# Loading q in two half-tile transfers with 512-byte runs, and restoring the token order in a PSUM copy

## The chip, the cores and the metric

One core of a Trainium2 chip runs the program. The metric is device time in microseconds. Executions of one kernel on one chip that count as fast spread by up to 1.5 percent. A run more than 1.5 percent above the fastest of its kernel is marked slow. The changed kernel and every experiment were timed in rounds beside the kernel before on the same chip. A ratio is taken from fast runs of the same rounds, so it is not quite the ratio of the medians quoted beside it. The bracket behind a ratio is its 95% interval.

## The reference

Linear attention with a decay per head (4 batches, 8 heads, 768 tokens, 64 elements), then a feed-forward layer on 3072 tokens. The reference works in blocks of 64 tokens; the kernel gets the same result in chunks of 128.

```python
for b in range(nb):
    intra = np.einsum('bhic,bhjc->bhij', qb, kb) * Dmask[None]
    intra = np.einsum('bhij,bhjd->bhid', intra, vb)
    inter = np.einsum('bhid,bhde->bhie', qb * lam_pow[None], kv_state)
    out[:, :, sl] = intra + inter
    kv_state = lam_block[None, :, None, None] * kv_state + np.einsum('bhsd,bhse->bhde', kb_dec, vb)
...
x = np.ascontiguousarray(attn_out.transpose(0, 2, 1, 3)).reshape(B * S, H * D)
h = x @ w_in                    # 512 -> 2048, then a smooth ReLU, then @ w_out
```

## The kernel before

There are 24 chunks. SyncE loads k, q and v of a chunk as [128 tokens, 8 heads, 64] float32. A head's 64 elements are 256 contiguous bytes in memory, so a load is 1024 runs of 256 bytes. GpSimd scales and casts q and k; q is turned by PE (first chunks) or by a DMA transpose; PE makes scores, applies them to v and adds the state; ScalarE copies the result as x^T into SBUF; then the two large matmul layers follow, six stages of 512 tokens.

```python
def f_load(c, x, wait):
    t = ld.tile([128, H, D], F32, name=f"x{x}f", tag=f"x{x}f")
    b, s0 = c // NCB, (c % NCB) * C
    d = nc.sync.dma_start(out=t, in_=(q, k, v)[x][b, :, s0:s0 + C, :].rearrange("h p d -> p h d"))
...
def f_x(c):                                     # x^T of a chunk, from PSUM
    nc.scalar.copy(out=xT[sx][:, :, off:off + C], in_=pot[c])
...
# the planner: each operation is entered with its cost; run_plan sorts all engines' instructions by it
add(("ld", it, x), "SP", 590, lambda ...: f_load(i, x, wait), [...], due=pos_ * 1e-3, dma=1190)
```

The order of every engine's instructions is fixed before the run, by a list scheduler inside the kernel that works with entered costs. "SP, 590" is the issue on SyncE in nanoseconds, "dma" the transfer. At run time each engine follows its order and waits where data are late: in the profile of this kernel ScalarE waits 16.4 us for v.

## Time and profile before

| | before |
|---|---|
| time, median of 2 runs | 229.81 us (228.67 to 230.96) |
| profiled span | 225.5 us |
| PE busy | 205.6 us, so 19.9 idle |
| 256 KB q load | 24 issues, median 4.4 us from issue to landing |
| k loads from chunk 10 on (the expectations below call it chunk 8) | (146.50 - 69.65) / 13 = 5.91 us apart |

The page's engine line gives busy time, share of the span and number of instructions; the stretches give, for each window, its length and every engine's busy time. The idle time of PE is what can be won or lost. The lines themselves stand in the prediction below.

### The profile page before, as it was taken

What the parts mean: (1) busy time and instruction counts of PE and PEld (TensorE: products, weight loads), DVE (VectorE), ACT (ScalarE), POOL (GpSimd) and SP (SyncE); (2) the same over time, 40 slices, a digit from 0 to 9 for tenths busy, and PEclk for the clock granted to TensorE, in tenths of its full rate; (3) what the DMA queues carried; (4) which work ended last, traced back from release to release, by engine and by line L of the source; (5) the groups of instructions that cost most, each with busy time, mean ns of one, the idle gap of its engine ahead of it and who ended that gap; (6) DMA issues with size and microseconds to landing.
All of it is one profiled execution on the core that took longest, in us unless ns stands there. A gap on an engine that the chain in (4) does not pass through costs nothing.

```text
span 225.5 us, 4385 instructions
## 1 busy us (share of the span) xinstructions
PE 205.6 (91%) x1733; PEld 123.4 (55%) x1760; DVE 144.2 (64%) x218; ACT 123.6 (55%) x220; POOL 61.0 (27%) x65
## 2 busy tenths in 40 slices
PE   0497989999999989689999999999999999999992
PEld 0376634765888577567664554545545544444441
DVE  7687399978498948567655956856656564554300
ACT  3346867544678285546757575676655444455121
POOL 6543560056034332423342542361000000000000
PEclk9999999999999999999999999999999999999998
DMA  6999999999898797999999999999011001110212
GB/s 121 216 218 170 195 189 202 200 223 196 212 202 158 182 215 169 205 173 204 225 196 237 214 166 233 232 211 211 0 49 47 24 22 49 47 47 16 77 67 77
DMA packets 102837, 34.38 MB, mean 152 GB/s; under 512 B 95136, under 2 KB 99744, under 8 KB 102816
## 3 DMA queue, kind: packets, MB, share of 16 engines
q1 hardware_dynamic: 97920, 29.90, 70.4%
q0 software_dynamic: 4752, 4.19, 12.2%
q8 instruction: 14, 0.23, 0.5%
q14 instruction: 7, 0.06, 0.1%
q10 hardware_dynamic: 144, 0.00, 0.0%
HBM read 27.27 MB, written 6.29 MB: 149 GB/s over the span
## 4 chain that ended last, share of the span: by engine, by line
PE 57%; SPq 3%; DMA 2%; issue 1%; ACT 1%; ACTq 0%
PE py L365 27%; PE ph L332 23%; PE po L305 3%; DMA x2f<-in_v_dram 2%; PE ps L285 2%; SPq L406 1%; PE po L302 1%; PE pu L266 1%; SPq L256 1%; SPq L260 1%; ACT vi L235 0%; ACT osb L370 0%; PE pt L285 0%; ACTq L370 0%
## 5 line engine op out<-in xcount | busy, mean ns | idle before, releaser
L332 PE MATMUL ph<-xT,w_in_sb 128*128 128x128 bf16 (+1 forms) x741 | 92.5, 268 | 1.9 <-ACT xT L312 1.0
L365 PE MATMUL py<-w_out_sb,gT 128*128 128x512 bf16 x368 | 92.6, 379 | 1.0 <-issue 0.2
L340 ACT ACTIVATE r<-ph,one 128x512 bf16<-128x512 f32 (+2 forms) x96 | 64.6, 678 | 47.7 <-PE ph L332 38.4
L332 PEld LDWEIGHTS <-w_in_sb 128*128 128x128 bf16 x752 | 52.5, 98 | 29.0 <-issue 2.2
L365 PEld LDWEIGHTS <-gT 128*128 128x128 bf16 x384 | 35.7, 98 | 38.8 <-DVE gT L356 0.2
L348 DVE TENSOR_SCALAR t<-r 128x1024 bf16<-128x1024 bf16 x48 | 25.2, 526 | 42.7 <-ACT r L340 42.7
L356 DVE TENSOR_TENSOR gT<-w,t 128x1024 bf16<-128x1024 bf16 x48 | 39.8, 828 | 1.6
L231 POOL TENSOR_TENSOR ks<-x1f,tab_k 128x512 bf16<-128x512 f32 x20 | 22.1, 1103 | 62.0 <-DMA x1f<-in_k_dram 48.9
L351 DVE TENSOR_TENSOR w<-r,t 128x1024 bf16<-128x1024 bf16 x48 | 37.2, 775 | 1.5
L231 POOL TENSOR_TENSOR qs<-x0f,tab_q 128x512 bf16<-128x512 f32 x24 | 28.5, 1189 | 25.7 <-DMA x0f<-in_q_dram 25.3
L235 ACT CAST vi<-x2f 128x512 bf16<-128x512 f32 x24 | 14.8, 616 | 16.5 <-DMA x2f<-in_v_dram 16.4
L295 DVE TENSOR_TENSOR sc<-ps,causal 128x512 bf16<-128x512 f32 x20 | 13.8, 689 | 13.6 <-PE pt L285 13.6
L370 ACT COPY osb<-py 128x512 f32<-128x512 f32 x24 | 14.1, 586 | 15.1 <-PE py L365 13.4
L305 PE MATMUL po<-sc,vi 128*128 128x128 bf16 x192 | 19.2, 226 | 0.2
L312 ACT CAST xT<-po 128x512 bf16<-128x512 f32 x24 | 14.0, 585 | 7.2 <-PE po L305 6.6
L270 ACT CAST ubd<-pu 64x256 bf16<-64x256 f32 x40 | 14.6, 364 | 5.3 <-PE pu L266 5.0
L305 PEld LDWEIGHTS <-vi 128*128 128x128 bf16 x192 | 15.2, 102 | 2.3 <-issue 0.6
L302 PE MATMUL po<-qT,ubd 128*128 128x128 bf16 x80 | 15.1, 224 | 0.0
L295 DVE TENSOR_TENSOR sc<-pt,causal 128x512 bf16<-128x512 f32 x20 | 13.6, 680 | 0.0
L266 PE MATMUL pu<-vi,ks 128*128 128x128 bf16 x80 | 8.4, 232 | 2.4 <-ACT vi L235 2.3
L241 PE MATMUL pt<-ident,ks 128*128 128x128 bf16 x24 | 3.1, 266 | 8.0 <-DVE ks L231 7.8
L266 PEld LDWEIGHTS <-ks 128*128 128x128 bf16 x80 | 6.4, 105 | 5.5 <-issue 3.1
(48 smaller groups left out, 87.4 us busy)
## 6 DMA issues: line engine op xcount, KB each, us to landing
x1f<-in_k_dram SPq DMA_DIRECT2D x24, 256.0 KB, 4.8
x0f<-in_q_dram SPq DMA_DIRECT2D x24, 256.0 KB, 4.4
x2f<-in_v_dram SPq DMA_DIRECT2D x24, 256.0 KB, 4.6
out_dram<-osb SPq DMA_DIRECT2D x24, 256.0 KB, 2.6
w_out_sb<-in_moe_w_out_dram POOLq DMA_DIRECT2D x4, 512.0 KB, 13.3
w_in_sb<-in_moe_w_in_dram POOLq DMA_DIRECT2D x3, 512.0 KB, 6.6
w_in_sb<-in_moe_w_in_dram POOLq DMA_DIRECT2D x2, 256.0 KB, 5.0
kT<-ks SPq DMA_TRANSPOSE x18, 4.2
```

Source lines behind the costliest of these rows:

```text
L231: eng.tensor_tensor(t, qkv_ld[c, x], _bc(tab[:, c % NCB, :], 2, D), op=AX.mult)
L235: nc.scalar.copy(out=v_out(vi[c % NV]), in_=qkv_ld[c, 2].rearrange("p (a b) d -> p a b d", b=2))
L266: nc.tensor.matmul(pu[0][:, hp, :], lhsT=pair(ks[c], hp), rhs=v_pair(vi[c % NV], hp), start=(c % NCB == 0 and hp == 0), stop=True, skip_gr ...
L295: nc.vector.tensor_tensor(sc_sb[c][:, g], pst[c, g], _bc(causal, 1, HP), op=AX.mult)
L302: nc.tensor.matmul(po[:, hp], lhsT=ubd[(c - 1) % NUB][:, hp, :], rhs=qT[c][:, hp, :], start=True, stop=False)
L305: nc.tensor.matmul(po[:, hp], lhsT=vi[c % NV][:, hp, hi].rearrange("p a d -> p (a d)"), rhs=sc_sb[c][:, hi, hp, :], start=(cb == 0 and hi ...
L332: nc.tensor.matmul(ph[:, j * m:(j + 1) * m], lhsT=w_in_sb[:, ko, (ni + j) * 128:(ni + j + 1) * 128], rhs=xT[s][:, ko, part * m:(part + 1) ...
L340: nc.scalar.activation(out=r_t[grp][:, i, cs], in_=ph_t[s, ni, part][:, cs], func=AF.Relu, bias=one[:, 0:1])
L348: nc.vector.tensor_scalar(t_t[grp], r, 0.5, 1.0, op0=AX.mult, op1=AX.min)
L351: nc.vector.tensor_tensor(w_t[grp], r, t_t[grp], op=AX.subtract)
L356: nc.vector.tensor_tensor(gT[s][:, f - RW * n:f, part * m:(part + 1) * m], w_t[grp].rearrange("p a (b m) -> p (a b) m", m=m), t_t[grp].rea ...
L365: nc.tensor.matmul(py_t[s, ms], lhsT=gT[s][:, ko, ms * 128:(ms + 1) * 128], rhs=w_out_sb[:, ko, :], start=(ko == 0), stop=(ko == FO - 1))
```

## The change

The intent: fewer and longer runs. Two neighbouring tokens of a head are 512 contiguous bytes. A chunk's q is loaded as 64 token pairs on 64 partitions for heads 0 to 3, and again on the other 64 partitions for heads 4 to 7. The cast puts even tokens before odd ones, the causal mask is built in that order, the matmuls read q as two runs of 64 columns, and the copy of x^T restores the order. The tables need lambda by half, which costs two more small loads. The planner gets 800 and 900 ns for a q load in place of 590 and 1190.

```diff
-    lam_b = const.tile([128, H], F32)
-    nc.scalar.dma_start(out=lam_b, in_=lam.partition_broadcast(128))
+    lam_b = const.tile([128, H + HL], F32)
+    nc.scalar.dma_start(out=lam_b[:, :H], in_=lam.partition_broadcast(128))
+    for g in range(2):
+        nc.scalar.dma_start(out=lam_b[64 * g:64 * g + 64, H:], in_=lam[g * HL:(g + 1) * HL].partition_broadcast(64))
...
+        if x == 0:
+            o = t.rearrange("p (e l) d -> p e l d", e=2)
+            i = i.rearrange("p (l e) d -> p e l d", e=2)
...
+    def q_cols(c, hp, rows=slice(0, 128)):
+        g, a = hp // 2, hp % 2
+        x = qT[c][rows, a, g * 64:(g + 1) * 64]
+        return bass.AP(x.tensor, x.offset, [list(x.ap)[0], [256, 2], [1, 64]])
...
-        nc.scalar.copy(out=xT[sx][:, :, off:off + C], in_=pot[c])
+        nc.scalar.copy(out=xT[sx][:, :, off:off + C].rearrange("p h (j e) -> p h j e", e=2),
+                       in_=pot[c].rearrange("p h (e j) -> p h j e", e=2))
...
+        if x == 0:
+            for g in range(2):
+                i = q[b, g * HL:(g + 1) * HL, s0:s0 + C, :].rearrange("l (j e) d -> j l (e d)", e=2)
+                d = nc.sync.dma_start(out=t[64 * g:64 * g + 64].rearrange("p (l e) d -> p l (e d)", e=2), in_=i)
...
-            add(("ld", it, x), "SP", 590, ... dma=1190)
+            add(("ld", it, x), "SP", 590 if x else 800, ... dma=1190 if x else 900)
```

More of the change, by code (lines that the diff above doesn't have):

```diff
@@ L89 @@
     nc.scalar.preload_act_table_set("natural_log_exp_and_others")
-    lam_b = const.tile([128, H], F32)
-    nc.scalar.dma_start(out=lam_b, in_=lam.partition_broadcast(128))
+    HL = H // 2
+    lam_b = const.tile([128, H + HL], F32)
+    nc.scalar.dma_start(out=lam_b[:, :H], in_=lam.partition_broadcast(128))
+    for g in range(2):
+        nc.scalar.dma_start(out=lam_b[64 * g:64 * g + 64, H:], in_=lam[g * HL:(g + 1) * HL].partition_broadcast(64))
     ident = const.tile([128, 128], BF16)
     make_identity(nc, ident)
-    ln_lam = const.tile([128, H], F32)
+    ln_lam = const.tile([128, H + HL], F32)
     nc.scalar.activation(out=ln_lam, in_=lam_b, func=AF.Ln)
-    pos_i = const.tile([128, NCB], I32)
-    nc.gpsimd.iota(pos_i, pattern=[[C, NCB]], base=-S // 2, channel_multiplier=1)
+    pos_i = const.tile([128, 3, NCB], I32)
+    nc.gpsimd.iota(pos_i[:, 0], pattern=[[C, NCB]], base=-S // 2, channel_multiplier=1)
+    for g in range(2):
+        nc.gpsimd.iota(pos_i[64 * g:64 * g + 64, 1:3], pattern=[[1, 2], [C, NCB]], base=-S // 2, channel_multiplier=2)
     causal = const.tile([128, 128], F32)
@@ L103 @@
         out=causal, in_=causal, compare_op=AX.is_ge, fill=0.0,
-        base=0, pattern=[[1, 128]], channel_multiplier=-1)
+        base=0, pattern=[[1, 2], [2, 64]], channel_multiplier=-1)
     NKB, NUB, NV = 3, 3, 4
@@ L112 @@
     nc.vector.memset(kbd[0], 0.0)
-    pos = const.tile([128, NCB], F32)
+    pos = const.tile([128, 3, NCB], F32)
     nc.vector.tensor_copy(pos, pos_i)
@@ L118 @@
         nc.gpsimd.memset(t, 0.0)
-    arg = const.tile([128, NCB, H], F32)
-    nc.vector.tensor_tensor(arg, _bc(pos, 2, H), _bc(ln_lam, 1, NCB), op=AX.mult)
+    arg = const.tile([128, NCB, 2, H], F32)
+    nc.vector.tensor_tensor(arg[:, :, 0], _bc(pos[:, 0], 2, H), _bc(ln_lam[:, :H], 1, NCB), op=AX.mult)
+    for e in range(2):
+        nc.vector.tensor_tensor(arg[:, :, 1, e * HL:(e + 1) * HL], _bc(pos[:, 1 + e], 2, HL),
+                                _bc(ln_lam[:, H:], 1, NCB), op=AX.mult)
+    tab_k = const.tile([128, NCB, H], F32)
+    nc.scalar.activation(out=tab_k, in_=arg[:, :, 0], func=AF.Exp, scale=-1.0)
     tab_q = const.tile([128, NCB, H], F32)
-    nc.scalar.activation(out=tab_q, in_=arg, func=AF.Exp)
-    tab_k = const.tile([128, NCB, H], F32)
-    nc.scalar.activation(out=tab_k, in_=arg, func=AF.Exp, scale=-1.0)
+    nc.scalar.activation(out=tab_q, in_=arg[:, :, 1], func=AF.Exp)
     for t in ubd + kbd[1:]:
@@ L230, in cast @@
         t = qkp.tile([128, H, D], BF16, name=nm, tag=nm)
-        eng.tensor_tensor(t, qkv_ld[c, x], _bc(tab[:, c % NCB, :], 2, D), op=AX.mult)
+        i = qkv_ld[c, x]
+        o, tb = t, _bc(tab[:, c % NCB, :], 2, D)
+        if x == 0:
+            o = t.rearrange("p (e l) d -> p e l d", e=2)
+            i = i.rearrange("p (l e) d -> p e l d", e=2)
+            tb = _bc(tab[:, c % NCB, :].rearrange("p (e l) -> p e l", e=2), 3, D)
+        eng.tensor_tensor(o, i, tb, op=AX.mult)
         d[c] = t
@@ L277, in f_s @@
                 nc.tensor.matmul(pst[c, g][:, 2 * hi + j, :], lhsT=kbd[c % NKB][:, 2 * g + j, hi, :],
-                                 rhs=qT[c][:, 2 * g + j, :], start=True, stop=True)
+                                 rhs=q_cols(c, 2 * g + j), start=True, stop=True)
     def f_s2(c):
@@ L284, in f_s2 @@
             for hi in range(2):
-                nc.tensor.matmul(pst[c, hi][:, hp, :], lhsT=kT[c][HD[hi], hp, :], rhs=qT[c][HD[hi], hp, :],
+                nc.tensor.matmul(pst[c, hi][:, hp, :], lhsT=kT[c][HD[hi], hp, :], rhs=q_cols(c, hp, HD[hi]),
                                  start=True, stop=True)
@@ L301, in f_o @@
             if cb > 0:
-                nc.tensor.matmul(po[:, hp], lhsT=ubd[(c - 1) % NUB][:, hp, :], rhs=qT[c][:, hp, :],
+                nc.tensor.matmul(po[:, hp], lhsT=ubd[(c - 1) % NUB][:, hp, :], rhs=q_cols(c, hp),
                                  start=True, stop=False)
@@ L405, in f_load @@
         b, s0 = c // NCB, (c % NCB) * C
-        d = nc.sync.dma_start(out=t, in_=(q, k, v)[x][b, :, s0:s0 + C, :].rearrange("h p d -> p h d"))
+        if x == 0:
+            for g in range(2):
+                i = q[b, g * HL:(g + 1) * HL, s0:s0 + C, :].rearrange("l (j e) d -> j l (e d)", e=2)
+                d = nc.sync.dma_start(out=t[64 * g:64 * g + 64].rearrange("p (l e) d -> p l (e d)", e=2), in_=i)
+        else:
+            d = nc.sync.dma_start(out=t, in_=(k, v)[x - 1][b, :, s0:s0 + C, :].rearrange("h p d -> p h d"))
         if wait is not None:
@@ L431 @@
         for x in (1, 0, 2):
-            add(("ld", it, x), "SP", 590, lambda i=it, x=x, wait=gated if x == 1 else None: f_load(i, x, wait),
-                [("cast", it - LD, x), ("w",) + w_seen[-2] if w_seen else None], due=pos_ * 1e-3, dma=1190)
+            add(("ld", it, x), "SP", 590 if x else 800, lambda i=it, x=x, wait=gated if x == 1 else None: f_load(i, x, wait),
+                [("cast", it - LD, x), ("w",) + w_seen[-2] if w_seen else None], due=pos_ * 1e-3, dma=1190 if x else 900)
             pos_ += 1
```

## The prediction

> **What bounds the kernel now.** I read the engine table and the slices first, then the busy time by stretches, then the chain of waits, then the timeline of the first 27 us and SyncE's issues.
>
> ```profile
> PE 205.6 (91%) x1733; PEld 123.4 (55%) x1760; DVE 144.2 (64%) x218; ACT 123.6 (55%) x220; POOL 61.0 (27%) x65
> ...
> DMA  6999999999898797999999999999011001110212
> ```
>
> PE is busy 205.6 of 225.5 us, so 19.9 us of idle PE is the most that any change of loads could win. The DMA row is at 9 for nearly all of the first 157 us, so the loads are a second resource that is almost full. Where do the 19.9 us lie?
>
> ```profile
> 0.00:22.50 22.50, 12.21 (x113) 10.16 (x114) 16.75 (x29) 10.34 (x22) 11.33 (x19) 1.00 1.13 181
> 22.50:60.00 37.50, 36.50 (x324) 22.07 (x327) 29.03 (x42) 22.31 (x41) 13.71 (x14) 1.00 1.18 201
> 60.00:100.00 40.00, 36.11 (x495) 28.65 (x500) 30.61 (x43) 24.89 (x47) 13.44 (x13) 1.00 0.99 190
> 100.00:155.00 55.00, 54.57 (x460) 31.30 (x467) 37.05 (x56) 35.52 (x63) 21.94 (x20) 1.00 1.21 212
> 155.00:185.00 30.00, 29.80 (x187) 14.79 (x190) 16.90 (x29) 16.19 (x27) 0.61 (x1) 1.00 0.20 47
> 185.00:225.50 40.50, 36.40 (x167) 16.39 (x168) 13.85 (x23) 14.30 (x22) 0.00 (x0) 0.98 0.14 53
> ```
>
> The first two numbers are the length and PE's busy time. PE idles 10.3 us in the prologue, 1.0, then 3.9 in the middle, 0.4, 0.2, and 4.1 at the end, most of it after the last matmul (about 221.6). After 100 us PE is full: whatever q's loads do there moves nothing. So the change can work on two places: the prologue, and the 3.9 us of the middle.
>
> The middle, in the chain of waits:
>
> ```profile
> 88.44 1.10 SPq L406
> 89.65 2.13 SPq L256
> 92.45 5.29 DMA x2f<-in_v_dram
> 97.74 0.02 issue
> 97.76 0.63 ACT vi L235
> 98.39 0.04 issue
> 98.43 0.38 PE pu L266 x4
> ```
>
> PE waited for v of a chunk, which SyncE issued late, behind a stretched load and a stretched transpose. PE's timeline shows gaps of about 1.0 us before 79.92, 1.7 to 2 us before 93.22 and 0.65 before 98.43: together 3.3 us that earlier loads could remove.
>
> The prologue:
>
> ```profile
> 8.33 1.14 SPq L406 DMA_DIRECT2D x0f<-in_q_dram  x1
> ...
> 9.52 1.10 SPq L406 DMA_DIRECT2D x2f<-in_v_dram  x1
> ...
> 13.54 1.04 POOL L231 TENSOR_TENSOR qs<-x0f,tab_q 128x512 bf16<-128x512 f32 x1 [2.57 <-DMA x0f<-in_q_dram]
> 13.93 1.20 DVE L231 TENSOR_TENSOR ks<-x1f,tab_k 128x512 bf16<-128x512 f32 x1
> ```
>
> Issues are held back to one in 1.19 us: a 256 KB load takes about that. GpSimd casts q at 6.40, 9.93, 13.54, 17.16, each on arrival, 3.6 us apart, three loads. But VectorE is busy 16.75 of 22.5 us and nearly without a gap from 11 us on; its k casts take 1.20 and 1.50 us beside a GpSimd cast and 0.63 without. Chunk 2's q was cast by 14.58 and transposed only at 17.27, when kbd was done. So the prologue is only partly bound by loads.
>
> [...] its packet records have a median of 18 ns for 256 bytes (14 GB/s per engine) and 85 ns for the 2048 bytes of a stored row (24 GB/s); it has no 512-byte packet of a plain load. [...] No load of before covers 64 partitions[...]. [...]
>
> **The change part by part.**
>
> *Transfer.* A q load is now 1024 runs of 256 bytes, 64 per engine: 64 x 18 = 1.15 us, near the 1.19 between issues. After: 512 runs of 512 bytes, 32 per engine. A line through the trace's 18 ns (256 B) and 85 ns (2048 B) gives 18 + 256 x 67/1792 = 27.6 ns, my estimate for one run: 32 x 27.6 = 0.88 us, 0.27 us less per chunk, 6.5 us of transfer in 24 chunks. [...] I expect about half: 0.15 us per chunk.
>
> *Issue.* 24 more issues on SyncE. A load's issue took 0.37 to 0.42 us when nothing stood ahead, 0.58 behind another, more when held back. I expect 0.4 to 0.6 us more per chunk. Per chunk SyncE needs at least 3 x 0.58 + 2 x 1.20 + 0.53 = 4.67 us, and from 69.65 to 111.82 the k loads come (111.82 - 69.65)/7 = 6.0 us apart. The rest is stretched issues (2.07, 2.13, 2.52 us) and waits. So the extra 0.5 us mostly fits in slack, but not before each load: v comes behind q in the order, and v is what PE waited for.
>
> *Setup.* Two more tiny loads of lambda on ScalarE's queue (0.42 us each), two iotas on GpSimd (0.13 each), two more products on VectorE (at most 0.21 each). The logarithm, now at 3.89 when its load lands, moves to about 4.8; VectorE's position cast ends at 4.67 (it runs as long as GpSimd's memsets), so the products end at about 5.5 instead of 5.00. Behind them are 1.85 us of memsets, then the first k cast, now 6.82: about 7.3. This is on the path: the first transposes start with it at 7.50.
>
> *Casts and copies.* The q cast reads runs of 64 in another order; same element count, 1.04 us, off the path. The score and state matmuls read q as two runs of 64 columns. The state product already reads v as two separate runs and its four matmuls start 55 ns apart (64.50 to 64.72), so no cost. The mask product is unchanged. The x^T copy reads PSUM in steps of 64 elements: 24 x 585 ns today; even at twice that ScalarE gains 14 us on 123.6 and stays under PE; the path sees it once or twice, up to 0.6 us.
>
> *Sum.* Prologue: +0.5 setup, minus what earlier q gives: 4 chunks x 0.15 = 0.6 at most in arrivals, half of it hidden by VectorE, -0.3; in addition some k casts may no longer meet a GpSimd cast. Net +0.1. Middle: chunks 0 to 13 are loaded before the last stall; 14 x 0.15 = 2.1 us of transfer freed, of which the order, the gate on the weights (SyncE waits 17.8 us for w_out) and the extra issues take more than half: -0.7 of the 3.3 us. Copy: +0.1. Total about -0.5 us on 229.8: 229.3.
>
> **The rivals.** (1) *Transfers bind throughout[...]*: 0.27 x 14 = 3.8 us earlier, all 3.3 us of the middle gone and 0.5 won in the prologue, 226.0. For it: the DMA row of nines, the prologue's even 1.19 us. Against it: in the 2 us stretches from 70 to 76 the DMA share falls to 0.63, 0.69 and 0.46, just before the first stall, so bandwidth was not what lacked there. (2) *SyncE's issues bind*: 0.5 us more per chunk over the eight chunks from 60 to 100 is 4 us later; minus what stretched issues absorb (about half), PE stalls 2 us more, and with the setup 232.3. For it: SyncE issues without a pause from 66 on, and stretched issues stand in the chain of waits. Against it: part of those stretches are back-pressure[...]. (3) *It is hidden*: PE, the setup and the weights' gate leave everything within 0.3 us, 229.8.
>
> One further risk: the order of all instructions is planned from the entered costs (800 ns issue and 900 ns transfer for q instead of 590 and 1190), so the order may shift elsewhere, either way by a microsecond.
>
> **Range and chances.** Centre 229.3. The rivals span 226.0 to 232.3; the two runs of before differ by 2.3 us themselves, so the range is 226.0 to 233.0. Faster by over 2% means under 225.2, below even rival 1, so it needs a lucky order as well: 0.05. Slower by over 2%, over 234.4, needs rival 2 without absorption: 0.11. The rest: 0.84.
>
> **What would show each step.** The transfer: q packets of 512 bytes with a median near 28 ns[...], and q casts in the prologue under 3.5 us apart. The issue: 48 q issues, SyncE's time per chunk from 66 to 112 still about 6 us, not 6.5. The setup: first k cast near 7.3, first PE work near 8. The copy: x^T still near 585 ns. The middle: PE's busy time in 60:100 above 36.1 by under 1 us, and 100:185 full as before. I am wrong if PE stalls after 100 us, if 60:100 loses more than 2 us, or if the prologue's start of the main matmuls (22.4) moves by more than 1 us.

## The result, and the profile after

The changed kernel took 240.73 us (239.11 to 242.34, 2 runs) against 229.81: ratio 1.0469 [1.0316, 1.0622]. It is slower by 4.7%, above the stated range of 226 to 233.

The page of the changed kernel, engine line and DMA row of the slices:

```profile
PE 206.5 (87%) x1760; PEld 122.4 (52%) x1760; DVE 141.2 (59%) x220; ACT 121.8 (51%) x220; POOL 62.4 (26%) x67
...
DMA  5999999999898999898999999989110111101212
```

PE works as long as before (206.5 against 205.6) in a span 11.9 us longer, so nearly all of the loss is idle PE. (Before's trace lacks 27 of 1760 matmul records, so its idle time is a little overstated.) The row of nines, the time in which loads run, fills 28 of the 40 slices in both, but a slice is now 5.94 us long and was 5.64: about 8 us more. The same stretches as before:

```profile
0.00:22.50 22.50, 10.16 (x108) 8.41 (x109) 13.73 (x30) 10.15 (x21) 11.25 (x21) 1.00 1.07 166
22.50:60.00 37.50, 35.87 (x316) 21.47 (x315) 25.50 (x40) 22.62 (x42) 14.57 (x14) 1.00 1.18 200
60.00:100.00 40.00, 34.03 (x477) 27.06 (x476) 27.84 (x40) 22.09 (x41) 12.87 (x12) 1.00 0.98 185
100.00:155.00 55.00, 50.39 (x445) 29.30 (x443) 36.22 (x51) 31.05 (x58) 19.77 (x19) 1.00 1.00 194
155.00:185.00 30.00, 27.37 (x190) 13.91 (x189) 16.84 (x26) 16.26 (x29) 3.90 (x3) 1.00 0.46 89
185.00:237.40 52.40, 48.73 (x241) 22.21 (x239) 21.11 (x35) 19.61 (x30) 0.00 (x0) 1.00 0.12 46
```

Length minus PE's busy time, after against before: 12.3 against 10.3, 1.6 against 1.0, 6.0 against 3.9, 4.6 against 0.4, 2.6 against 0.2, 3.7 against 4.1. More than half of the loss, 6.6 us, lies after 100 us, where PE was full before. Who waited there? In the list of waits from 100 to 185 us (total us, times, longest) one line of before, ScalarE's cast of v:

```profile
ACT vi L235 <- DMA x2f<-in_v_dram: 3.6, 6, 0.9
```

and of after, the same cast and the three longest waits of PE:

```profile
ACT vi L249 <- DMA x2f<-in_v_dram: 27.8, 11, 4.4
...
PE ph L353 <- ACT r L361: 2.9, 4, 1.0
...
PE pu L286 <- ACT vi L249: 2.2, 2, 1.4
PE ph L353 <- ACT xT L332: 1.6, 1, 1.6
```

v is loaded behind q. Over the whole execution it comes late 21 times in 24 (13 times before), and ScalarE waits 42.4 us for it (16.4 before). ScalarE keeps its order, so what stands behind the cast of v is late too. The longest such wait in the timeline:

```profile
165.26 0.62 ACT L249 CAST vi<-x2f 128x512 bf16<-128x512 f32 x1 [4.37 <-DMA x2f<-in_v_dram]
...
166.04 0.68 ACT L361 ACTIVATE r<-ph,one 128x512 bf16<-128x512 f32 x1
...
166.78 1.02 PE L353 MATMUL ph<-xT,w_in_sb 128*128 128x512 bf16 x4 [1.01 <-ACT r L361]
```

Seven of PE's eight waits after 100 us, 6.7 of 7.2 us, end within 2.1 us of the start of such a late cast; the eighth is for the turned q (0.54). Loads also come further apart: k loads start at 71.93 for chunk 10 (numbering from 0) and at 156.01 thirteen chunks later, (156.01 - 71.93) / 13 = 6.47 us apart instead of 5.91. This distance alone does not set the time, as the planned orders below show.

Two things about the q load itself. First its issue, before and then after (the tile's SyncE line: count, then duration in ns as minimum, median, maximum):

```profile
L406 SPq DMA_DIRECT2D x0f<-in_q_dram x24: 425/581/2530, 1.3 to 149.7; - x24
```

```profile
L430 SPq DMA_DIRECT2D x0f<-in_q_dram x48: 601/621/2595, 1.3 to 158.6; - x48
```

Half the bytes take no less to issue; a pair in the steady stretches takes 1.28 us. Second the transfer. The changed kernel's timeline in the prologue:

```profile
8.01 2.83 SPq L430 DMA_DIRECT2D x0f<-in_q_dram  x2
8.17 0.63 DVE L245 TENSOR_TENSOR ks<-x1f,tab_k 128x512 bf16<-128x512 f32 x1
...
10.69 1.30 POOL L245 TENSOR_TENSOR qs<-x0f,tab_q 128x512 bf16<-128x512 f32 x1 [2.95 <-DMA x0f<-in_q_dram]
...
14.79 1.04 POOL L245 TENSOR_TENSOR qs<-x0f,tab_q 128x512 bf16<-128x512 f32 x1 [2.79 <-DMA x0f<-in_q_dram]
```

q arrives 4.1 us apart, not 3.6 as before, and the issue of this pair is held back to 2.83 us. Half-microsecond stretches there (last number: GB/s) show the dip:

```profile
7.50:8.00 0.50, 0.00 (x0) 0.00 (x0) 0.44 (x2) 0.47 (x1) 0.24 (x1) 1.00 1.34 201
8.00:8.50 0.50, 0.00 (x0) 0.00 (x0) 0.50 (x2) 0.15 (x1) 0.00 (x0) 1.00 1.26 123
8.50:9.00 0.50, 0.15 (x2) 0.15 (x3) 0.29 (x1) 0.00 (x0) 0.00 (x0) 1.00 1.23 174
```

Before, the same part of the prologue runs at 213 to 226 GB/s. While halves are loaded, the rate falls to 123. The records of single packets say the same: the 512-byte packets that start from 8.0 to 8.5 us take 83 ns in the mean, against 28 to 31 from 7.5 to 8.5 us in the run below that has one load of all partitions.

### The profile page after: what moved, and what is told of

Its sections match the earlier page's. A ratio compares the mean times of both kernels' runs of the same rounds, so it can differ in the third digit from the quotient of the medians.

```text
span 237.4 us, 4450 instructions
## 1 busy us (share of the span) xinstructions
PE 206.5 (87%) x1760; PEld 122.4 (52%) x1760; DVE 141.2 (59%) x220; ACT 121.8 (51%) x220; POOL 62.4 (26%) x67
## 5 line engine op out<-in xcount | busy, mean ns | idle before, releaser
L353 PE MATMUL ph<-xT,w_in_sb 128*128 128x128 bf16 (+1 forms) x752 | 93.7, 270 | 7.3 <-ACT r L361 3.4
L386 PE MATMUL py<-w_out_sb,gT 128*128 128x512 bf16 x384 | 95.4, 379 | 0.0
L369 DVE TENSOR_SCALAR t<-r 128x1024 bf16<-128x1024 bf16 x48 | 23.5, 489 | 43.5 <-ACT r L361 43.4
L377 DVE TENSOR_TENSOR gT<-w,t 128x1024 bf16<-128x1024 bf16 x48 | 40.4, 843 | 1.5
L245 POOL TENSOR_TENSOR ks<-x1f,tab_k 128x512 bf16<-128x512 f32 x20 | 23.4, 1168 | 65.4 <-DMA x1f<-in_k_dram 41.4
L372 DVE TENSOR_TENSOR w<-r,t 128x1024 bf16<-128x1024 bf16 x48 | 38.2, 796 | 1.5
L249 ACT CAST vi<-x2f 128x512 bf16<-128x512 f32 x24 | 14.8, 618 | 42.8 <-DMA x2f<-in_v_dram 42.4
L245 POOL TENSOR_TENSOR qs<-x0f,tab_q 128x512 bf16<-128x512 f32 x24 | 28.3, 1177 | 29.4 <-DMA x0f<-in_q_dram 27.6
L325 PE MATMUL po<-sc,vi 128*128 128x128 bf16 x192 | 18.5, 223 | 0.1
L325 PEld LDWEIGHTS <-vi 128*128 128x128 bf16 x192 | 14.7, 100 | 1.7 <-issue 0.2
L322 PE MATMUL po<-qT,ubd 128*128 128x128 bf16 x80 | 14.5, 219 | 0.0
L305 PE MATMUL ps<-qT,kT 64*128 64x128 bf16 x80 | 7.8, 217 | 3.4 <-DMA qT<-qs 3.4
```

What stands on the lines that cost most here:

```text
L245: eng.tensor_tensor(o, i, tb, op=AX.mult)
L249: nc.scalar.copy(out=v_out(vi[c % NV]), in_=qkv_ld[c, 2].rearrange("p (a b) d -> p a b d", b=2))
L322: nc.tensor.matmul(po[:, hp], lhsT=ubd[(c - 1) % NUB][:, hp, :], rhs=q_cols(c, hp), start=True, stop=False)
L325: nc.tensor.matmul(po[:, hp], lhsT=vi[c % NV][:, hp, hi].rearrange("p a d -> p (a d)"), rhs=sc_sb[c][:, hi, hp, :], start=(cb == 0 and hi ...
L353: nc.tensor.matmul(ph[:, j * m:(j + 1) * m], lhsT=w_in_sb[:, ko, (ni + j) * 128:(ni + j + 1) * 128], rhs=xT[s][:, ko, part * m:(part + 1) ...
L369: nc.vector.tensor_scalar(t_t[grp], r, 0.5, 1.0, op0=AX.mult, op1=AX.min)
```

## The experiments

There were 18 kernels in five calls; those of one call shared a chip and the runs of before, whose medians were 227.5 to 228.7 us. Theories: the second issue on SyncE; the slow half transfers (a load of partitions 0 to 63 or 64 to 127 moves more slowly than one of all; the expectations call it the port theory, a name for my guess at the cause: no trace and no run here shows a port); the planned order; the setup with lambda.

**Parts of the load alone, on the kernel before, in the order of before.** Two loads of all partitions, four heads each:

```diff
+        for g in range(2 if x == 0 else 1):
+            hs = slice(0, H) if x else slice(g * HP, g * HP + HP)
+            d = nc.sync.dma_start(out=t[:, hs], in_=(q, k, v)[x][b, hs, s0:s0 + C, :].rearrange("h p d -> p h d"))
```

> The kernel before, with q in two loads of all 128 partitions, four heads each, runs of 256 bytes as before; the planned order is untouched. It doubles q's issues[...]. Issue theory (SyncE's 0.7 us more per chunk is what the change lost): k loads from chunk 8 on come about 6.4 us apart instead of 5.9, PE idles in 100 to 185, and the time is 1.025 to 1.05 of before. Port theory (halves of the partitions are slow): q casts in the prologue stay 3.6 us apart, the time is under 1.015 of before. Order theory (the new plan): within 1 percent of before.

Measured: 230.14 us, 1.0141 [1.006, 1.0221]. k loads 6.21 us apart, q casts in the prologue still 3.6. The second issue costs 1.4%; the issue theory had said 2.5 to 5, so it is a part and not the whole.

Two loads of 64 partitions, eight heads each, still 256-byte runs:

```diff
+        for g in range(2 if x == 0 else 1):
+            ps = slice(0, C) if x else slice(g * 64, g * 64 + 64)
+            d = nc.sync.dma_start(out=t[ps], in_=...[x][b, :, s0 + ps.start:s0 + ps.stop, :].rearrange("h p d -> p h d"))
```

> The kernel before, with q in two loads of 64 partitions, eight heads each, runs of 256 bytes; planned order untouched. As many issues and bytes as the run by heads; only which partitions one load reaches differs. Issue theory: the same time as the run by heads, within 0.5 percent. Port theory: in the prologue the rate falls below 160 GB/s while q moves (it is 215 to 220 before), the q casts come 4.0 us apart or more instead of 3.6, and the time is at least 1 percent above the run by heads.

Measured: 235.73 us, 1.0368 [1.0298, 1.0439]: 2.2% above the run by heads, with as many issues, runs and bytes. q casts come 3.7 to 3.9 us apart, and k loads 6.48. The time is as the port theory said; the prologue's dip is milder than it said (casts under 4.0 apart, 180 GB/s in the lowest half microsecond). A pair's issue is also longer, 1.30 us against 1.12; a single one took at least 0.60 us on 64 partitions and 0.37 on 128, with 512 runs of 256 bytes in both.

Is it the issue or the transfer? The same two kernels with the second load issued from ScalarE's queue:

```diff
-            d = nc.sync.dma_start(out=t[...], ...)
+            d = (nc.scalar if g else nc.sync).dma_start(out=t[...], ...)
```

> The kernel before, q in two loads of 128 partitions and four heads each, the second issued from ScalarE's queue instead of SyncE's. SyncE has then as many issues as before; ScalarE, 55 percent busy, gets 24 more. If the 1.4 percent of the run by heads is SyncE's issue time: back to 0.995 to 1.006 of before, k loads from chunk 8 on 5.9 us apart (6.2 by heads). If it is something else in having two loads (the transfers, the semaphores): stays at 1.01 to 1.02.

Measured: 227.64 us, 1.001 [0.9963, 1.0058]; k loads 5.79 us apart. That is as the issue theory expected: with the second issue off SyncE the cost of the run by heads is gone.

> The same with halves of the partitions: two loads of 64 partitions, the second issued from ScalarE's queue. If the 2.3 percent between halves and heads is the longer issue (1.29 us a pair against 1.12), it goes away with the issue: within 0.5 percent of the run by heads with ScalarE's queue. If it is the slower transfer of a half[...]: it stays 1 to 2.5 percent above that run, and the rate in the prologue dips under 205 GB/s while q moves.

Measured: 234.92 us, 1.034 [1.0259, 1.042], above the expected 1 to 2.5% over the run by heads. Stretches of the prologue, by heads and then by halves, both with ScalarE's queue:

```profile
7.50:8.00 0.50, 0.49 (x5) 0.50 (x6) 0.00 (x0) 0.00 (x0) 0.00 (x0) 1.00 1.25 226
8.00:8.50 0.50, 0.50 (x6) 0.27 (x3) 0.35 (x1) 0.00 (x0) 0.00 (x0) 1.00 1.35 224
```

```profile
7.50:8.00 0.50, 0.50 (x5) 0.50 (x6) 0.00 (x0) 0.00 (x0) 0.00 (x0) 1.00 1.44 160
8.00:8.50 0.50, 0.50 (x6) 0.27 (x3) 0.35 (x1) 0.00 (x0) 0.00 (x0) 1.00 1.40 144
```

The engines are at nearly the same work; the rate differs, 224 to 226 against 144 to 160 GB/s. In the packet records of this microsecond a 256-byte packet takes 22 to 25 ns in the mean by heads and 37 to 40 by halves. So loads of a half are slow as transfers. Most of the 3.4% is special to this form: ScalarE issues its loads late, in its own order, and loads after the weights resume at 46.87 instead of 43.56 by heads. Of the 7.8 us more of idle PE than by heads, 5.1 lie before 60 us, where halves issued by SyncE lost nothing (11.9 us idle against 13.9 by heads). After 60 us the halves cost 2.8 us, 1.2%.

Does it matter which 64 partitions? Both loads put on partitions 0 to 63, or both on 32 to 95, for chunks from 6 on (wrong result, relative errors 0.07 and 0.10):

```diff
+        if x == 0 and c >= LD:
+            for g in range(2):
+                d = nc.sync.dma_start(out=(x0s[c % LD] if g else t)[0:64], ...)     # or [32:96]
```

> The kernel before, with q of the chunks from 6 on in two loads of 64 partitions; wrong result on purpose: both loads go to partitions 0 to 63 (the second to a spare buffer that nothing reads; the cast reads what chunk c-6 left in the other rows). Chunks 0 to 5 load as before, so the prologue is unchanged; planned order of before. Partner of the run with partitions 32 to 95. Both theories expect about 1.02 to 1.035 of before (18 of 24 chunks with the costs of the run by halves, 1.037; a little less because the cast waits only for the first load).

> The same, with both loads to partitions 32 to 95: as many partitions, bytes, runs and issues[...]. Port theory: at least 1 percent faster than with partitions 0 to 63, near 1.010 to 1.015 (the run by heads), and k loads about 0.2 us per chunk closer. Rival (64 partitions are slow in themselves, or the longer issue of such a load does it): the same time within 0.5 percent.

Measured: 236.33 us, 1.0399 [1.0331, 1.0468], and 233.80 us, 1.0246 [1.019, 1.0303]. By these ratios the upper set is 1.5% faster with the same number of partitions, runs and issues. The gap is less sure than the intervals look: one run of the first kernel is slow, and the fast runs, 234.03 to 237.48 and 232.32 to 234.31 us, overlap, with means 0.9% apart (235.57 and 233.56). The packet records are clearer. Of the 256-byte packets that start from 44 to 170 us, 1928 take over 40 ns with partitions 0 to 63 and 405 with 32 to 95; in before they are 604, by heads 594, by halves 1269. So in these two profiles the time of packets goes with which 64 partitions the loads reach; by what mechanism was not shown. What it costs in time is open: k loads are as far apart (6.46 and 6.44 us), and the two profiled executions took the same time (234.03 and 234.31). The run with 32 to 95 also stays 1% above the run by heads; the longer issue of a 64-partition load, 0.62 us, may be why, which no run tested.

**Longer runs alone, on the changed kernel.** One load of all partitions with 512-byte runs (wrong result, relative error 0.08; the right one would need a source of four dimensions in one load, which no run tried):

```diff
-            for g in range(2):
-                i = q[b, g * HL:(g + 1) * HL, s0:s0 + C, :]...
+            i = bass.AP(qa.tensor, qa.offset, [[2 * D, 128], [S * D, HL], [1, 2 * D]])
+            d = nc.sync.dma_start(out=t.rearrange("p (l e) d -> p l (e d)", e=2), in_=i)
```

> The changed kernel with q in ONE load of 128 partitions and 512-byte runs. Wrong result on purpose: it reads 128 pairs of tokens of four heads in place of 64 pairs of eight, as many bytes and runs. Everything else as in the changed kernel. It takes away the second issue and the halves, and keeps runs, order and setup. Issue and port theories: back to within 1 percent of before or under it (0.985 to 1.01), with q casts in the prologue under 3.5 us apart. Order or setup theory: stays 1.03 to 1.05 of before.

Measured: 227.91 us, 1.0025 [0.9947, 1.0104]. Without second issue and halves the loss is gone, although order and setup of the change stayed. Two stretches of its prologue, one as q moves and one as k and v move:

```profile
8.00:8.50 0.50, 0.00 (x0) 0.00 (x0) 0.50 (x4) 0.49 (x3) 0.00 (x0) 1.00 1.20 290
...
9.50:10.00 0.50, 0.00 (x0) 0.00 (x0) 0.44 (x3) 0.00 (x0) 0.30 (x2) 1.00 1.30 222
```

While the longer runs move the rate is 290 GB/s, and from the second on q casts come 3.2 to 3.3 us apart. Yet the kernel is no faster than before. With the lambda loads away and the costs of before entered:

> The one load of 512-byte runs of all partitions (wrong result on purpose, as before), now without the two extra loads of lambda and with the entered costs of before, so planned as before. The run without these two mends was 1.0025. If the longer runs are worth something that setup and order had hidden: 0.985 to 0.995 of before. If the time freed on the transfers is hidden anyway behind PE and SyncE: 0.997 to 1.003.

Measured: 225.51 us, 0.9902 [0.9851, 0.9952]. So 512-byte runs in one load are worth about 1% in this order, where nothing else is paid for them.

**The planned order.** The changed kernel with before's entered costs:

```diff
-  "SP", 590 if x else 800, ... dma=1190 if x else 900
+  "SP", 590, ... dma=1190
```

> The changed kernel, with the entered costs of a q load put back to 590 and 1190 ns, so that the planner orders all engines as before. Order theory: it wins back most of the 4.7 percent, 1.00 to 1.02 of before. Issue and port theories: it stays at 1.035 to 1.055 of before.

Measured: 234.72 us, 1.0329 [1.0268, 1.039]. Neither theory fits well: part of the loss goes, most stays (the interval reaches the 1.035 of the issue and port theories). The kernel before with the costs of the change:

> The kernel before with the entered costs of a q load as in the changed kernel (800 ns issue, 900 ns transfer), nothing else. Order theory: the planned order is worse in itself, 1.005 to 1.02 of before. If the 1.4 percent between the changed kernel in its own order and in the order of before comes only from the mismatch of the costs with the true ones (about 1.28 us and 1.5 us), it should show here too, since here they are 0.58 and 1.19. If it was noise between chips: within 0.5 percent.

Measured: 234.26 us, 1.0269 [1.0196, 1.0342]. This is more than I expected of the order: with not one byte of its loads changed, it loses 2.7%. In its timeline, PE's largest wait after the prologue is

```profile
33.77 1.46 PE L332 MATMUL ph<-xT,w_in_sb 128*128 128x512 bf16 x4 [3.42 <-DMA w_in_sb<-in_moe_w_in_dram]
```

a wait for weights of 3.42 us that the order of before has not. By the traces SyncE's order here is that of the changed kernel, which waits only 0.67 us at this place, so this wait is not what the order costs there. Then costs nearer to the changed trace: a pair's issue takes 1.27 us there (at 100.61), and 1700 ns is an estimate, within the 1.5 to 2.1 us that 256 KB take at the 174 to 123 GB/s of the dip:

```diff
+  "SP", 590 if x else 1270, ... dma=1190 if x else 1700
```

> The changed kernel with the entered costs of a q load set to what its trace shows, 1270 ns of issue and 1700 ns of transfer. If the 1.4 percent between its own order and the order of before comes from entering too low costs: at or under the run with the costs of before, 1.02 to 1.034 of before. If any order but the tuned one loses: 1.035 to 1.06.

Measured: 230.22 us, 1.0094 [1.0031, 1.0158]. That looked like a mismatch between entered and true costs, cured. The test is the same pair of numbers in the kernel before, for which they are far too high (there a q load takes 0.58 us to issue in the median, and loads come 1.19 us apart in the prologue):

> The kernel before, with 1270 ns of issue and 1700 ns of transfer entered for a q load, which truly costs 0.58 and 1.19. Mismatch theory (an order planned for loads that come earlier than they do stalls PE; the cure is true costs): too high costs are no gain here, 0.997 to 1.015 of before. Rival (the order of the run a_trueplan is luckier or more cautious for any kernel): faster than before, 0.985 to 0.995.

Measured: 226.58 us, 0.988 [0.9791, 0.997]. The mismatch theory falls: too high costs make before faster as well. In the stretch from 60 to 100 us that kernel has

```profile
60.00:100.00 40.00, 39.52 (x543) 31.41 (x548) 30.75 (x44) 25.75 (x46) 12.47 (x11) 1.00 0.91 185
```

so PE idles 0.5 us there and not 3.9. The profiled execution (227.58 us) is no faster than that of before (227.32), though: it idles 1.3 us more in the prologue, 1.8 more from 22.5 to 60 and 1.6 more from 100 to 155. The gain is that of the timed runs. By the traces 89 of SyncE's 132 loads, transposes and stores stand at another place in its sequence than before. ScalarE's wait for v over the whole execution, in the changed kernel with 1270 and 1700 and in the kernel before with them:

```profile
ACT vi L249 <- DMA x2f<-in_v_dram: 12.2, 11, 2.6
```

```profile
ACT vi L235 <- DMA x2f<-in_v_dram: 2.2, 2, 2.0
```

So v is far less late in these orders (42.4 and 16.4 us of waiting without them), although k loads are further apart than before, 6.69 and 6.18 us. That v is the way by which they gain is likely, but which of the moved instructions does it was not tested.

Which of the two numbers matters?

```diff
a_issueplan:  "SP", 590 if x else 1270, ... dma=1190 if x else 900
a_xferplan:   "SP", 590 if x else 800,  ... dma=1190 if x else 1700
```

> The changed kernel with only the issue cost set right (1270 ns); the transfer stays at the 900 ns of the change. Own order 1.047, both set right 1.009. If SyncE's issue time is what was missing in the plan: 1.005 to 1.02. If the transfer's 1.7 us is: 1.03 to 1.05.

> The changed kernel with only the entered transfer time set to 1700 ns, the issue left at the 800 ns of the change. Issue alone set right gave 1.048, both 1.009. If the entered transfer time is what matters: 1.005 to 1.02. If both are needed together: 1.03 to 1.05.

Measured: 238.85 us, 1.0479 [1.0415, 1.0542], and 228.70 us, 1.0054 [0.9989, 1.0119]. Of the two it is the transfer time that matters (by the traces SyncE's order at 800 / 1700 is that at 1270 / 1700). At 1700 the changed kernel comes within 1% of before; at 900 it is the worst, whatever the issue.

**The setup.** The changed kernel without the two extra loads of lambda:

```diff
-    nc.scalar.activation(out=ln_lam, in_=lam_b, func=AF.Ln)
+    nc.scalar.activation(out=ln_lam[:, :H], in_=lam_b[:, :H], func=AF.Ln)
+    for g in range(2):
+        nc.scalar.activation(out=ln_lam[64 * g:64 * g + 64, H:], in_=lam_b[64 * g:64 * g + 64, g * HL:(g + 1) * HL], func=AF.Ln)
```

> The changed kernel without its two extra loads of lambda: the logarithms of each half's four heads are taken from the first load, on the same partitions. If the setup is on the path (first k cast at 8.17 instead of 6.82 in the profiles): the first k cast comes back to about 7.0 and the time falls by 0.3 to 0.6 percent against the changed kernel, to 1.03 to 1.045 of before. If the slow loads hide it: no change, 1.047.

> The changed kernel with both true costs entered and without the two extra loads of lambda. a_trueplan was 1.009. If the later setup (first k cast at 8.17 instead of 6.82) costs once the order no longer hides it: 0.998 to 1.005. If the prologue is bound by q's loads anyway: 1.006 to 1.012.

Measured: 239.26 us, 1.0511 [1.0461, 1.0561] in the order of the change: no gain. In the order of 1270 and 1700: 228.58 us, 1.0005 [0.9901, 1.0108], against 1.0094 with the loads, in another call; the intervals overlap, so a gain there is not shown.

**A version that has the longer runs without the halves.** From chunk 6 on, q of two chunks is loaded at once: 128 token pairs on 128 partitions, 512 KB, 512-byte runs. Each chunk reads its own 64 columns of the turned q. The result is correct.

```diff
+        if x == 0 and c >= PQ:                                   # PQ = 6, even chunks only
+            t = qkv_ld[c, x] = ld2.tile([128, H, 2 * D], F32, name="x0p", tag="x0p")
+            nc.sync.dma_start(out=t, in_=q[b, :, s0:s0 + 2 * C, :].rearrange("h (j e) d -> j h (e d)", e=2))
...
+        x = qT[c][rows, 0, hp, (c % 2) * 64:(c % 2) * 64 + 64]
+        return bass.AP(x.tensor, x.offset, [list(x.ap)[0], [HP * 128, 2], [1, 64]])
```

> The kernel before, with q of the chunks from 6 on loaded for two chunks at once: one load of 512 KB, 128 pairs of tokens on all 128 partitions, 512-byte runs, correct result. It halves q's issues and has the longer runs without halves of the partitions; the token order is restored in the x^T copy as in the change. Costs 590 and 1900 ns entered. If the gain of a_one512_lam (0.990) comes from the transfers after the prologue: 0.985 to 0.995. If it came from the prologue's loads, or the pair's later cast (2.1 us, both chunks at once) eats it: 0.997 to 1.01.

Measured: 228.84 us, 1.0046 [0.9987, 1.0104]: no gain. With longer entered transfers (1700 for chunks 0 to 5, 2700 for a pair):

> The two-chunk load (correct result) with longer entered transfers: 1700 ns for a q load of chunks 0 to 5, 2700 for a pair, issue 590. If an order that expects q later is good for any form of the load, and the 512-byte runs add something of their own: 0.975 to 0.988 of before, under b_trueplan. If the order is the whole of it: 0.985 to 0.995. If the order suits only single loads: 0.997 to 1.01.

Measured: 225.96 us, 0.9861 [0.9771, 0.9951]. This and the kernel before with 1270 and 1700 entered (0.988) are the two correct versions that beat both kernels. They were not run in one call and their intervals overlap; the second is an edit of two numbers.

## Why the prediction was wrong

Put side by side, the ratios to before by kernel and entered costs (issue / transfer, ns):

| entered | kernel before | changed | changed over before, same entry |
|---|---|---|---|
| 590 / 1190 | 1 | 1.033 | 1.033 |
| 800 / 900 | 1.027 | 1.047 | 1.047 / 1.027 = 1.020 |
| 1270 / 1700 | 0.988 | 1.009 | 1.009 / 0.988 = 1.022 |

In these three orders the load with its setup costs 2 to 3.3%; each ratio is uncertain by about one percent. The order that came with it cost the kernel before 2.7% and the changed kernel 1.4% (1.047 / 1.033). With one load of all partitions, order and setup together cost 1.2% (1.0025 / 0.9902 = 1.012). So what the order costs depends on the load, and the two losses do not simply add.

**Transfer.** The step that failed: "I expect about half: 0.15 us per chunk", as a gain. The single-packet part was right over the whole execution: 512-byte packets have a median of 27 ns in the records (27.6 estimated). But in the first 24 us their median is 46 ns, with 123 GB/s at the lowest while q moves and q casts 4.1 us apart instead of 3.6. So the term was -0.15 us per chunk and measured about (4.1 - 3.6) = +0.5 in the prologue. Even no gain at all would have been too kind. No load of before covers 64 partitions, so its trace told nothing of how half loads move; taking half of the 0.27 us as a gain was a guess.

**Issue.** "0.4 to 0.6 us more per chunk" was 0.70 (1.28 against 0.58). "Mostly fits in slack" failed: by heads alone, with 0.54 us more of issue, k loads went from 5.91 to 6.21 us apart and the time rose 1.4%. Rival 2, SyncE's issues, was thus real (its 232.3 is 1.1%), but alone it gave only 1.4%; ScalarE's queue removes it (1.001).

**Order.** The other step that failed: "the order may shift elsewhere, either way by a microsecond". The entered 800 and 900 alone moved the kernel before by 2.7% of 228.0, about 6 us. Even added to the top of the range, 233, this gives 239 and does not reach the 240.73.

**"After 100 us PE is full: whatever q's loads do there moves nothing."** Wrong as a rule. 6.6 us of new idle PE appear after 100 us, nearly all of it behind a cast of v that came late. A full engine shows that a gain is worth nothing there; it does not show that a delay costs nothing. It is not that all loads end later: with 1270 and 1700 entered the changed kernel starts its last k load at 159.14, after the 156.01 here, and PE idles 3.5 us from 100 to 185 instead of 7.2.

**Setup.** Mechanism right, size too small: the logarithm ran at 5.70 (4.8 predicted), the first k cast at 8.17 (7.3). That it is on the path is not shown: taking it away gained nothing in the order of the change.

**Casts and copies.** Right. The x^T copy with its steps of 64 in PSUM:

```profile
L332 ACT CAST xT<-po x24: 577/586/606, 14.9 to 191.5; 128x512 bf16<-128x512 f32 x24
```

is as before (mean 588 against 585 ns), and the state products that read q as two runs keep 219 ns.

**The middle and the signs.** Of the three gaps that the prediction counted as 3.3 us for earlier loads, the first (0.97 us before 79.92) ended with ScalarE's x^T copy in the trace and not with v. The stretch lost 2.1 us instead of gaining 0.7 (PE busy 34.03 against 36.11). Of the three signs of being wrong two came, this one and the stalls after 100 us; the main matmuls started at 22.79 instead of 22.44, within the stated 1 us.

**What stays open.** How much of the halves' loss is the slower transfer rather than the longer issue of such a load, and what slows that transfer; and why an order that expects q later is better for the kernel before too. The runs show that it is, and by which number, but not through which instructions; that v is less late in it is seen, not tested.

## What to carry to other kernels

When a change alters the costs on which a static schedule is computed, test the new costs on the old kernel first: here they alone lost 2.7%, and a wrong but larger number won 1.2%. Split a load by a free dimension and not by partitions (1.014 against 1.037 here), and count each extra issue against the issuing queue's cycle: here 0.54 us more per chunk cost 1.4%, although the queue's issues were already stretched (1.14 us in the prologue of before against 0.58). Read an engine that is full as a limit on gains only: here 6.6 us of new idle time came where PE had been full.
